# Two filler tiles in SBUF: the operands of TensorE at multiples of 256 bytes

## The chip, the core and the metric

The kernel runs on one core of a Trainium2 chip. The metric is device time in microseconds (us) of one execution; lower is better. The profile shows one execution, taken by the hardware profiler.

## What is computed

Block-causal attention over 4 x 8 heads of 576 positions, then two feed-forward stages over all 2304 tokens. Cut to what matters:

```python
# q, k, v: (4, 8, 576, 64) float32
scores = (1/8) * q @ k.T                      # masked where block(i) < block(j), block = 64
attn = exp(scores - max); attn = attn / (sum(attn) + 1e-9)
x = (attn @ v) -> (2304, 512)
x = (1 / (1 + exp(-(x @ w_gate))) * (x @ w_val)) @ w_out     # 512 -> 1536 -> 512
h = x @ w_in;  out = maximum(0.01 * h, h) @ w_out2            # 512 -> 2048 -> 512
```

## The kernel before

Everything is held transposed: features on the 128 partitions, tokens along the free dimension. The feed-forward products are made of float32r matmuls of 128 x 128 weights against up to 512 tokens. For accuracy every operand is split into a high part and a low part, and a product is three matmuls: high by high, high by low, low by high. So each streamed tile and each weight tile `w` holds two halves, and a unit of four 128-row pieces is 12 matmuls into one PSUM tile (L1296 to L1302 in `half_unit`).

The tokens are worked through in three slices. The first has 768 tokens in two parts of 256 and 512; its `x` lies in `xa` (256) and `x0` (512). The second has 512 tokens, in `x1`. The last two slices of 512 run as a pair, by a scheme of seven block products instead of eight (`pair_unit`, L1123), each product being two groups of three matmuls (L1146 to L1150); its streamed blocks lie in whatever is free by then: `both`, `x1`, `xa`, `g`, `qk`, `raw`, `acc` and `sg`. Weights are in `w`, a ring of seven buffers of 4096 bytes in each partition.

Attention of batch 0 comes first, that of the others is interleaved with the feed-forward work of the first two slices. Scores take both operands from `qk` (L426), transposes use `both` and `ident` (L567, L631), and the products with `v` stream the transposed probabilities from `both` (L655). These are full fp32 matmuls, which stand in the trace as two records each.

A planner (`Plan.order`, L149) orders the operations of all engines by due times and by costs that it works out from shapes; it knows no addresses. Rings and single tiles are reserved in the order in which the code opens their pools, from L263 on, each tile rounded up to 32 bytes. `warm` is a tile of one column that serves to load the Exp table early (L1454 to L1456); it is made in the pool `const`, which comes first in memory.

Of the kernel before, what the change touches and what calls it, by code (L numbers as in the profile page):

```python
# [8 lines left out]
F32 = mybir.dt.float32  # L9
# [4 lines left out]
AF = mybir.ActivationFunctionType  # L14
# [4 lines left out]
P = 128  # L19
# [205 lines left out]
def block_attention_then_two_mlps(  # L225
# [13 lines left out]
    nc = tc.nc  # L239
# [16 lines left out]
    def pool(name, bufs, **k):  # L256
        return ctx.enter_context(tc.tile_pool(name=name, bufs=bufs, **k))

    def ring(name, bufs, shape, dtype=F32, **k):
        return Ring(pool("p_" + name, bufs, **k), bufs, shape, dtype, name)  # L260

    out_hbm = out
    const = pool("const", 1)  # L263
# [20 lines left out]
    ident = const.tile([P, P], F32, name="ident")  # L284
    mask = const.tile([P, 4 * P + BLK], BF16, name="mask")
    x1 = const.tile([P, 4, 2, TN], F32R, name="x1")
    r_x = ring("x0", 4, [P, 2 * TN])
    r_xa = ring("xa", 2, [P, 4 * CUT])
    x0, xa, xt = [r_x.tile(F32R) for _ in range(4)], [r_xa.tile(F32R) for _ in range(2)], []
# [1159 lines left out]
    with tc.manual_schedule():  # L1449
        make_identity(nc, ident)  # L1450
        nc.gpsimd.memset(p_l[BLK:, (NKT - 1) * P:], 0.0)
        nc.gpsimd.memset(mask, 0.0)
        nc.gpsimd.memset(mask[:BLK, 4 * P:], MASK)
        warm = const.tile([P, 1], F32, name="warm")  # L1454
        nc.vector.memset(warm, 0.0)
        nc.scalar.activation(warm, warm, AF.Exp)  # L1456
        for o, e in plan.order():
            for t in o.uses:
                if t.ap is None:
                    t.ap = t.ring.pool.tile(t.ring.shape, t.dtype, name=t.ring.name)  # L1460
            if o.either:
                o.fn(e)
            else:
                o.fn()
# [39 lines left out]
```

## Time and profile before

| | us |
|---|---|
| median of 3 runs (lowest, highest) | 995.12 (994.21, 996.48) |
| the profiled execution | 994.91 |
| its span | 993.1 |
| TensorE busy | 977.9 |
| TensorE's weight loads busy | 779.7 |
| VectorE busy | 779.5 |
| ScalarE busy | 550.3 |
| GpSimd busy | 166.1 |

A matmul's end is modelled in this profile, and matmuls overlap: one lasts longer than the distance to the next. How fast TensorE goes is read from the starts, so the rows below are mostly of the timeline, which gives the start of a group of like matmuls, the time from its first start to its last end, and their number.

### The profile page before, as it was taken

The page shows a single profiled execution, that of the slowest core. Times are in us where ns is not written, and L with a number is a line of the kernel's source. Part 1 is how long each engine was busy: PE and PEld are TensorE (multiplying, and loading weights), DVE is VectorE, ACT ScalarE, POOL GpSimd, SP SyncE. Part 2 cuts the span into 40 slices and gives each one's busy share as a digit, 9 for nine tenths or more (in the row PEclk, how much of TensorE's full clock was granted, in tenths as well). Part 3 has the DMA queues.
Part 4 walks back from the last instruction along what each step waited for, and adds up shares of the span by engine and source line. Part 5 has one row for each costly group of instructions (what it writes and reads, how often), then busy time and mean ns, then how long its engine had stood idle before and what let it go on. Part 6 is the DMA issues. An engine that isn't in the chain of part 4 may idle for free.

```text
span 993.1 us, 15675 instructions
## 1 busy us (share of the span) xinstructions
PE 977.9 (98%) x5468; PEld 779.7 (79%) x5468; DVE 779.5 (78%) x1658; ACT 550.3 (55%) x1103; POOL 166.1 (17%) x172
## 2 busy tenths in 40 slices
PE   7999999999999999999999999999999999999998
PEld 4688888878888878778777777788888877888886
DVE  6989989889989847777689888966437489958656
ACT  7988776676766526464566565443525144643521
POOL 2422001221102001232332223021002021100000
PEclk9999999999999999999999999999999999999999
DMA  8499786756876537979997877876565555665554
GB/s 207 135 292 270 264 289 219 258 186 242 265 258 197 208 116 268 299 273 298 281 296 266 303 265 243 280 267 220 173 200 186 187 170 160 204 204 182 193 185 154
DMA packets 92718, 227.52 MB, mean 229 GB/s; under 512 B 9952, under 2 KB 29920, under 8 KB 92640
## 3 DMA queue, kind: packets, MB, share of 16 engines
q1 hardware_dynamic: 92640, 226.53, 69.5%
q8 instruction: 43, 0.70, 0.3%
q14 instruction: 35, 0.29, 0.1%
HBM read 150.47 MB, written 76.02 MB: 228 GB/s over the span
## 4 chain that ended last, share of the span: by engine, by line
PE 94%; DVE 3%; DMA 1%; ACT 1%; SPq 0%; issue 0%; POOL 0%; DVEq 0%; ACTq 0%
PE mm L1299 48%; PE sc L1147 17%; PE tp L1147 9%; PE mm L1147 4%; PE tp L631 3%; PE sc L426 3%; PE pa L655 2%; PE tp L426 2%; PE tp L567 1%; DMA qk<-in_qk 1%; PE mm L655 1%; PE tp L582 1%; DMA w<-ds 1%; DVE x L1219 0%; SPq L330 0%; DVE g L353 0%
## 5 line engine op out<-in xcount | busy, mean ns | idle before, releaser
L1299 PE MATMUL mm<-x,w 128*128 128x512 f32 (+2 forms) x1008 | 236.9, 387 | 0.0
L1299 PEld LDWEIGHTS mm<-x,w 128*128 128x128 f32 x1008 | 179.8, 188 | 40.8 <-issue 5.2
L1299 PE MATMUL mm<-g,w 128*128 128x512 f32 (+1 forms) x792 | 164.0, 358 | 0.0
L1299 PEld LDWEIGHTS mm<-g,w 128*128 128x128 f32 x792 | 130.0, 189 | 23.4 <-issue 2.3
L1147 PE MATMUL sc<-both,w 128*128 128x512 f32 x480 | 130.6, 396 | 0.1
L1147 PEld LDWEIGHTS sc<-both,w 128*128 128x128 f32 x480 | 90.1, 188 | 21.8 <-ACT wf L340 0.5
L498 ACT ACTIVATE both<-both,nm 128x256 f32<-128x256 f32 (+5 forms) x148 | 84.1, 570 | 29.7 <-DVE nm L483 29.1
L899 POOL TENSOR_TENSOR wf<-mag,rnd 128x512 int32<-128x512 int32 x28 | 37.4, 1335 | 204.3 <-DVE w L353 149.5
L885 ACT ACTIVATE mag<-raw 128x512 f32<-128x512 f32 x68 | 45.5, 670 | 43.9 <-DVE wf L899 18.0
L1299 PE MATMUL mm<-xa,w 128*128 128x256 f32 x480 | 62.7, 281 | 0.0
L1299 PEld LDWEIGHTS mm<-xa,w 128*128 128x128 f32 x480 | 59.9, 188 | 3.3 <-issue 0.8
L353 DVE TENSOR_TENSOR g<-gf,g 128x512 fp32r<-128x512 f32 (+2 forms) x73 | 57.8, 793 | 3.5 <-ACT g L340 3.4
L518 POOL TENSOR_SCALAR both<-both,r 128x256 f32<-128x256 f32 (+6 forms) x54 | 34.9, 652 | 116.4 <-DVE r L511 97.0
L340 ACT ACTIVATE g<-gf 128x512 fp32r<-128x512 f32 (+2 forms) x61 | 40.0, 657 | 23.6 <-DVE gf L1330 11.9
L516 ACT ACTIVATE both<-both,r 128x384 f32<-128x384 f32 (+6 forms) x94 | 48.6, 566 | 6.9 <-DVE r L511 6.9
L483 DVE CUSTOM_DVE_ANT_0 both<-sc,mask 128x256 f32<-128x256 f32 (+6 forms) x101 | 39.4, 423 | 15.9 <-PE sc L426 15.8
L1360 DVE TENSOR_TENSOR acc<-mm,acc 128x512 f32<-128x512 f32 (+1 forms) x60 | 35.7, 598 | 18.1 <-PE mm L1299 17.7
L1219 DVE TENSOR_TENSOR x<-sc,x 128x512 f32<-128x512 f32 x44 | 30.2, 689 | 23.2 <-PE sc L1147 23.2
L426 PE MATMUL sc<-qk 64*128 64x384 f32 (+5 forms) x228 | 42.2, 415 | 5.9 <-DMA qk<-in_qk 5.9
L893 DVE SCALAR_TENSOR_TENSOR mag<-raw,mag 128x512 int32<-128x512 int32 x68 | 47.4, 698 | 0.3
L1299 PE MATMUL mm<-sg,w 128*128 128x512 f32 (+1 forms) x216 | 47.4, 355 | 0.0
L353 DVE TENSOR_TENSOR w<-wf,w 128x512 fp32r<-128x512 f32 x68 | 46.5, 684 | 0.2
(255 smaller groups left out, 1851.0 us busy)
## 6 DMA issues: line engine op xcount, KB each, us to landing
w<-wd SPq DMA_DIRECT2D x102, 512.0 KB, 4.6
raw<-in_w SPq DMA_DIRECT2D x68, 512.0 KB, 4.5
wd<-w SPq DMA_DIRECT2D x68, 512.0 KB, 4.2
ds<-raw SPq DMA_DIRECT2D x68, 512.0 KB, 5.2
w<-ds SPq DMA_DIRECT2D x68, 512.0 KB, 4.3
qk<-in_qk SPq DMA_DIRECT2D x32, 288.0 KB, 6.3
w<-wd SPq DMA_DIRECT2D x68, 128.0 KB, 3.8
v<-in_v SPq DMA_DIRECT2D x32, 160.0 KB, 3.5
```

Of the source, the lines that this page charges most:

```text
L340: nc.scalar.activation(dst(), src(), AF.Copy)
L353: engines[e].tensor_tensor(dst(), a(), f32(b()), ALU.subtract)
L426: nc.tensor.matmul(ps[row:row + nq, col:col + nk], lhsT=tqk[half, 0, q0:q0 + nq], rhs=tqk[half, 1, k0:k0 + nk], start=True, stop=True,)
L483: nc.vector.tensor_tensor_reduce(out=pt[:, n:n + width], in0=ps[:, col:col + width], in1=mask[:, 4 * P + BLK - width:] if masked else mask ...
L498: nc.scalar.activation(pt[:, :n], pt[:, :n], AF.Exp, bias=nm[:, k - 1:k], scale=-1.0, accum_out=sm[:, i:i + 1],)
L516: nc.scalar.activation(pt[:, :n], pt[:, :n], AF.Copy, scale=r[:, i:i + 1])
L885: op("act", c_act(n), lambda: nc.scalar.activation(mag[:], words(1).bitcast(F32), AF.Abs), [raw], [mag], [raw, mag], d - 8)
L893: op("dve", c_dve(n), lambda: nc.vector.scalar_tensor_tensor(out=mag[:].bitcast(I32), in0=words(1).bitcast(I32), scalar=-0x40000000, in1=m ...
L899: engines[e].tensor_tensor(wf[:].bitcast(I32), mag[:].bitcast(I32), rnd[:], ALU.add)
L1147: nc.tensor.matmul(p[:, :n], lhsT=wt[:, wl, at * P:(at + 1) * P], rhs=view[:, xl], start=first and k == 0 and wl + xl == 0, stop=k == 1 an ...
L1299: nc.tensor.matmul(ps[:, :n], lhsT=ws[:, wl, k * P:(k + 1) * P], rhs=srcs[k]()[:, xl, hs], start=k == 0 and wl + xl == 0, stop=k == 3 and ...
L1360: op("dve", c_dve(n), lambda: nc.vector.tensor_tensor(a(), ps[:, :n], a(), ALU.add), [ps], toks_a, [ps, *host], e)
```

## The change

`warm` grows from 1 column to 64 (from 4 bytes, rounded to 32, to 256) and is made right after `x1`, where it stood already in memory. A new tile `even` of 48 columns (192 bytes), which nothing reads or writes, stands between the small rings `nm`, `sm`, `r` and the ring `x0`: its pool is opened there. No instruction is added, taken away or moved; the two that use `warm` name its first column.

```diff
     ident = const.tile([P, P], F32, name="ident")
     mask = const.tile([P, 4 * P + BLK], BF16, name="mask")
     x1 = const.tile([P, 4, 2, TN], F32R, name="x1")
+    warm = const.tile([P, 64], F32, name="warm")
+    pool("even", 1).tile([P, 48], F32, name="even")
     r_x = ring("x0", 4, [P, 2 * TN])
...
-        warm = const.tile([P, 1], F32, name="warm")
-        nc.vector.memset(warm, 0.0)
-        nc.scalar.activation(warm, warm, AF.Exp)
+        nc.vector.memset(warm[:, :1], 0.0)
+        nc.scalar.activation(warm[:, :1], warm[:, :1], AF.Exp)
```

Where the tiles start in a partition (byte, and its residue modulo 256):

| tile | before | residue | after | residue |
|---|---|---|---|---|
| `last`, `ident`, `mask` | 16512, 19072, 19584 | 128 | the same | 128 |
| `x1` | 20736 | 0 | 20736 | 0 |
| `raw`, `mag`, `rnd`, `wf` | from 37152 | 32 | from 37376 | 0 |
| `w` | from 63776 | 32 | from 64000 | 0 |
| `g`, `gf` | from 92448 | 32 | from 92672 | 0 |
| `qk`, `v` | from 126240 | 32 | from 126464 | 0 |
| `x0`, `xa` | from 145760 | 96 | from 146176 | 0 |
| `sg`, `both`, `acc` | from 170336 | 96 | from 170752 | 0 |

Within these tiles the operands start at multiples of 256 bytes, save for the second half of the last queries' scores in batch 0 (column 288), so a tile's residue is that of its operands.

## Rows read from the trace of the kernel before

**Rows 1.** The page, span and busy time of each engine (share of the span, instructions):

```profile
span 993.1 us, 15675 instructions
...
PE 977.9 (98%) x5468; PEld 779.7 (79%) x5468; DVE 779.5 (78%) x1658; ACT 550.3 (55%) x1103; POOL 166.1 (17%) x172
```

**Rows 2.** The page, the chain that ended last, by engine:

```profile
PE 94%; DVE 3%; DMA 1%; ACT 1%; SPq 0%; issue 0%; POOL 0%; DVEq 0%; ACTq 0%
```

**Rows 3.** Busy time by stretch: first slice, second slice, paired stage:

```profile
core 0: us, PE busy (x) PEld busy (x) DVE busy (x) ACT busy (x) POOL busy (x), PEclk, DMA share, GB/s
...
60.00:364.00 304.00, 303.65 (x1982) 257.87 (x1982) 263.71 (x597) 200.67 (x406) 39.68 (x34) 1.00 0.71 237
364.00:655.00 291.00, 289.87 (x1616) 220.81 (x1613) 243.24 (x521) 163.88 (x331) 77.82 (x81) 1.00 0.81 271
655.00:985.00 330.00, 328.28 (x1413) 264.44 (x1412) 221.75 (x346) 135.69 (x225) 29.38 (x22) 1.00 0.59 193
```

**Rows 4.** Waits of TensorE, longest first: total us, times, longest:

```profile
PE sc L426 <- DMA qk<-in_qk: 5.9, 3, 4.6
PE tp L1147 <- DMA w<-ds: 1.1, 1, 1.1
...
PE pa L426 <- DMA qk<-in_qk: 0.2, 1, 0.2
```

**Rows 5.** Weight loads by line and shape: count, busy us, mean ns, idle before:

```profile
L1299 PEld LDWEIGHTS mm<-x,w 128*128 128x128 f32 x1008 | 179.8, 188 | 40.8 <-issue 5.2 <-ACT gf L1343 0.3 <-DVE mag L889 0.2
L1147 PEld LDWEIGHTS sc<-both,w 128*128 128x128 f32 x480 | 90.1, 188 | 21.8 <-ACT wf L340 0.5 <-DVE v L1180 0.3 <-DVE x L1219 0.3
```

**Rows 6.** Timeline, paired stage: start us, us, engine, line, names, shapes, count:

```profile
723.99 0.85 PE L1147 MATMUL sc<-qk,w 128*128 128x512 f32 x3
724.67 0.84 PE L1147 MATMUL tp<-g,w 128*128 128x512 f32 x3
725.35 0.84 PE L1147 MATMUL sc<-raw,w 128*128 128x512 f32 x3
726.03 0.84 PE L1147 MATMUL sc<-qk,w 128*128 128x512 f32 x3
726.71 0.84 PE L1147 MATMUL mm<-raw,w 128*128 128x512 f32 x3
727.39 0.86 PE L1147 MATMUL sc<-acc,w 128*128 128x512 f32 x3
```

**Rows 7.** Timeline, paired stage, with `both` and `xa` streamed:

```profile
746.81 0.87 PE L1147 MATMUL sc<-both,w 128*128 128x512 f32 x3
747.51 0.86 PE L1147 MATMUL tp<-xa,w 128*128 128x512 f32 x3
748.21 0.86 PE L1147 MATMUL sc<-both,w 128*128 128x512 f32 x3
748.91 0.86 PE L1147 MATMUL tp<-xa,w 128*128 128x512 f32 x3
```

**Rows 8.** First slice, a run from `g`: timeline, then lengths min/median/max:

```profile
232.23 5.83 PE L1299 MATMUL mm<-g,w 128*128 128x512 f32 x25
...
L1299 PE MATMUL mm<-g,w x22: 389/389/389, 232.7 to 237.4; 128*128 128x512 f32 x22
```

**Rows 9.** Second slice, a run from `x1`: timeline, then lengths min/median/max:

```profile
375.20 5.52 PE L1299 MATMUL mm<-x,w 128*128 128x512 f32 x23
...
L1299 PE MATMUL mm<-x,w x22: 392/395/397, 375.4 to 380.3; 128*128 128x512 f32 x22
```

**Rows 10.** Timeline, first slice, a run from `x0`:

```profile
246.08 3.14 PE L1299 MATMUL mm<-x,w 128*128 128x512 f32 x13
```

**Rows 11.** Timeline, first slice, runs of 256 columns:

```profile
191.43 1.48 PE L1299 MATMUL mm<-g,w 128*128 128x256 f32 x11
...
103.69 1.34 PE L1299 MATMUL mm<-xa,w 128*128 128x256 f32 x10
...
259.29 1.07 PE L1299 MATMUL mm<-xa,w 128*128 128x256 f32 x8
```

**Rows 12.** Timeline, first slice, a unit from `g` right after 256 columns:

```profile
192.87 2.91 PE L1299 MATMUL mm<-g,w 128*128 128x512 f32 x12
```

**Rows 13.** Attention's transposes and products with `v`: count, busy us, mean ns:

```profile
L631 PE MATMUL tp<-ident,both 128*128 128x128 f32 x304 | 42.8, 274 | 0.8 <-ACT both L340 0.8
...
L655 PE MATMUL pa<-both,v 128*64 128x384 f32 (+3 forms) x192 | 26.2, 415 | 0.0
L567 PE MATMUL tp<-ident,both 128*128 128x128 f32 (+1 forms) x80 | 13.2, 276 | 0.3 <-ACT both L340 0.2
L655 PE MATMUL mm<-both,v 128*64 128x256 f32 (+1 forms) x96 | 10.4, 352 | 0.4 <-DVE both L342 0.3
```

## The prediction

> **What bounds the kernel now.** I read the busy line first, then the chain that ended last, the stretches, and TensorE's own waits. TensorE is busy 977.9 us of a span of 993.1 us [rows 1], the chain runs through it for 94% [rows 2], and its granted clock is 1.00 in every stretch [rows 3]. Its longest wait is the first load of q and k (5.9 us); every other wait that the view lists is at most 1.1 us [rows 4]. So the end is set by how many matmuls there are and by how closely they follow each other. The change adds none and moves none, so only the second can move.
>
> The change touches addresses alone, and the question is whether the trace shows an address in the distance from one matmul to the next (the pitch). It does, and this is the core of the argument. A row of the timeline that merges n matmuls covers n-1 pitches and the length of the last one. Before the change all weight tiles `w` lie at residue 32 (the byte in the partition, modulo 256), while the streamed operands lie at three residues:
>
> - `g`, `raw`, `qk` at 32, the same as `w`. From 723.99 on, five groups of three matmuls start exactly 0.68 us apart while the streamed tile goes from `qk` to `g`, `raw`, `qk` and `raw` [rows 6], so 226.7 ns each. The run of 25 from `g` gives the same: (5.83 - 0.39)/24 = 226.7, with every length at 389 ns [rows 8].
> - `both` and `xa` at 96, the same distance from `w`. Their groups start 0.70 us apart [rows 7], so 233.3 ns.
> - `x0`, also at 96: (3.14 - 0.39)/12 = 229.2 ns [rows 10]. So residue 96 has more than one settled pitch.
> - `x1` at 0, the only streamed buffer that is aligned already: (5.52 - 0.395)/22 = 233.0 ns [rows 9], with lengths of 392 to 397 ns.
>
> The weight loads last 188 ns under all of these [rows 5], so a load is not what became longer. Each lies inside a matmul's pitch, and its read of `w` runs beside the read of the streamed tile. What separates the good buffers from the others is that they lie a multiple of 256 bytes from `w`. `qk` is the useful case: its second half starts 2304 bytes after its first, which is 256 modulo 512, and it still runs at 0.68 us a group. So agreement modulo 256 is enough.
>
> **The change part by part.** The larger `warm` and the new `even` cost no instruction: the memset and the one Exp still work on one column. They take 640 bytes of each partition, and nothing is queued anew, so both are priced at 0. The order of instructions on every engine is the same.
>
> What they do is to bring `w`, `g`, `raw`, `qk`, `x0`, `xa`, `sg`, `both` and `acc` to residue 0, where `x1` lies. All streamed operands of the split products then agree with `w` modulo 256, as `g`, `raw` and `qk` do today. My forecast takes that agreement to be what counts, and prices every matmul as `g` behaves now. `g` does not reach 226.7 at once: after a switch of width its pitches are 233, 236, 229, 232, 231, 227 and then 226.7, and the row of twelve shows the mean, (2.91 - 0.39)/11 = 229.1 ns [rows 12]. That costs some 28 ns a restart, and I charge it to each.
>
> - Paired stage, 655 to 985 us, 1413 matmuls [rows 3]. From the starts of all of them, 1404 pitches are under 250 ns and sum to 324.8 us, a mean of 231.4; between 226.7 [rows 6] and 233.3 [rows 7] the mix of buffers gives about that. TensorE is hardly interrupted here, so nearly all settle: 1404 x (226.8 - 231.4) = **-6.4 us**.
> - Second slice, 364 to 655 us. 431 such pitches stream `x1`, at a mean of 233.2; attention work cuts into most units, so `g`'s mean with restarts (228.3) is what they get: 431 x -4.9 = -2.1 us. `g`, `sg` and `xa` together lose another 0.8 us. **-2.9 us**.
> - First slice, 60 to 364 us. It alternates between 256 and 512 columns. At 256 columns the settled pitch is (1.48 - 0.28)/10 = 120 ns for `g`, (1.34 - 0.28)/9 = 118 for `xa`, and elsewhere (1.07 - 0.28)/7 = 113 for the same `xa` [rows 11]. So agreement with `w` is no gain at this width, and the restart at each switch takes what 512 columns would win: `g` needs 1.43 + 2.75 us for a pair of units and `x0` with `xa` 1.41 + 2.75. **-0.5 us**, in truth nothing. If the 113 became the rule here, this term would be -6.5.
> - Attention's own matmuls in full fp32. Scores take both operands from `qk`, so their distance stays. Products of probabilities with `v` go from 64 apart to a multiple of 256, and transposes from 32 apart (`ident` at 128, `both` at 96) to 128. The trace has no equal shapes at two distances here. The large groups of these add up to 42.8 + 26.2 + 13.2 + 10.4 = 92.6 us [rows 13]; at the ratio of 233.3 to 226.7, 2.9%, that is 2.7 us either way, and the sign is open. I take 0, since rows 7 and 10 show that a distance alone doesn't fix the pitch.
> - Transfers and the other engines meet shifted addresses as well. No row separates these by residue. TensorE waits for transfers 5.9 + 1.1 + 0.2 = 7.2 us [rows 4]; a quarter of it, 2 us either way, is the bound, and I take 0.
>
> Sum: -6.4 - 2.9 - 0.5 = -9.8 us on TensorE. Not all of it reaches the end. In the first two slices VectorE is busy 87% and 84% [rows 3], and a faster TensorE will meet its results later. I take off 1.5 us, half of what is won there, and get -8.3. The profiled execution took 994.91 us for its span of 993.1, and the median of the runs is 995.12, so the two agree to 0.2 us and the forecast is **986.8 us**, 0.8% faster.
>
> The distance between two operands should by one rule not matter at all. The Trainium skill, TensorE: Matmul & The Clock Gate, section "Step-by-step: what each phase is for", says that "Loading the next tile's weights doesn't steal SBUF read bandwidth from the running matmul", since the two have a read port each. Rows 6 to 10 show pitches that differ by buffer, so something in the addresses acts; by that rule it would have to be the streamed buffer's own address, and that is the second rival below.
>
> **The rivals.** *Own address (slower).* If the streamed operand's own residue sets the pitch, then 32 is good, 96 middling and 0 the worst, and the change moves everything to 0. For this: `x1` is the one aligned buffer and runs at 233.0 [rows 9]. Against it: pitches keep changing for some six matmuls after a change of buffer or a restart [rows 12], and `x0` and `both` have the same residue with 229 and 233 [rows 7, 10], so a second stream is in play. Its price is each stretch at 233.2 ns for 512 columns: 1404 x 1.8 = +2.5, the second slice +1.4, the first +2.3, together +6.2 us: **1001 us**. It decides as soon as more than about half of the 512-column matmuls settle at `x1`'s pitch.
>
> *Nothing changes.* Several settled pitches exist per distance, so the new common distance may settle on another of them, or on a mixture whose mean is the present 231: **995 us**, 2 us either way. The Trainium skill, SBUF — State Buffer, in the note on cachelines under "Door 1: The DMA port swizzle", knows lines of 16 bytes only, and all buffers stand at a multiple of 16 already, so by it the filler does nothing. The pitches by residue [rows 6 to 10] speak against that as the whole story. That the tiles do not land where they should can be excluded: every address in the changed kernel is a multiple of 256 except for `ident`, `last` and `mask`, which stay at 128.
>
> *Eaten by the others.* TensorE gains 9.8 us, but in the first two slices all of it is waited away, and a third of the paired stage's share as well: -6.4 x 2/3 = -4.3, so **991 us**. For it: VectorE's 87%. Against it: waits that TensorE shows now are almost none [rows 4].
>
> **How the numbers follow.** The forecast has a chance of 0.57, eaten by the others 0.10, nothing changes 0.13, own address 0.20. About 0.2%, or 2 us, is what a measurement of this kernel can tell from no change. Faster by more is 0.57 + 0.10 = 0.67, within 0.13, slower 0.20. The forecast's own range is 982 to 991 us: -8.3 with 2.7 for attention and 2 for transfers on either side. To leave out no more than two in ten, the range has to reach into the slower case: 981 to 1000 leaves out some 0.04 below and 0.12 above.
>
> **What would show it.** In the paired stage, groups of three should start 0.68 us apart whatever they stream, and matmuls from `both`, `xa` and `x` should last 389 ns instead of 396; in the second slice settled runs from `x` should show 226.7. If they show 233 everywhere, `g` and `raw` too, then own address was right. If the pitches fall and the span doesn't, the waits of TensorE will have grown. The forecast is wrong altogether if agreement modulo 256 was only a by-product of residue 32, or if the pitch settles at a third value. The weight load should stay at 188 ns.

## The result

The changed kernel takes 986.67 us, median of 4 runs (985.49 to 987.15), beside 995.65 us of the kernel before; the ratio is 0.991, 95% interval 0.9892 to 0.9927. The forecast was 986.8. The kernel before had a median of 995.12 us of three runs when the forecast was made, and the fourth run moved it to 995.65; so the change measured is 9.0 us, where 8.3 were forecast.

The page of the changed kernel answers [rows 1]: TensorE is busy 9.4 us less with the same number of matmuls, and the span is 9.4 us shorter.

```profile
span 983.7 us, 15675 instructions
...
PE 968.5 (98%) x5468; PEld 780.4 (79%) x5468; DVE 777.4 (79%) x1658; ACT 549.6 (56%) x1103; POOL 163.1 (17%) x172
```

Busy time by stretch, columns as in [rows 3]. The stretches begin and end at the same matmuls as those of before, and so lie a little earlier:

```profile
59.10:363.90 304.80, 304.45 (x1983) 259.15 (x1983) 263.80 (x597) 200.86 (x406) 39.65 (x34) 1.00 0.71 236
363.90:652.00 288.10, 286.30 (x1616) 220.95 (x1613) 241.64 (x521) 163.51 (x331) 75.00 (x81) 1.00 0.81 274
652.00:975.80 323.80, 322.21 (x1412) 264.13 (x1411) 221.33 (x346) 135.31 (x225) 29.26 (x22) 1.00 0.61 197
```

The first slice went from 304.0 to 304.8 us, the second from 291.0 to 288.1, the paired stage from 330.0 to 323.8. Ahead of them stand 59.1 us instead of 60.0, behind them 7.9 instead of 8.1. The first of these is the wait for the first loads, which differs from execution to execution: a second profile of the changed kernel has 59.8 there.

The timeline of the paired stage, first the stretch of [rows 6], then that of [rows 7]:

```profile
719.12 0.84 PE L1149 MATMUL sc<-qk,w 128*128 128x512 f32 x3
719.80 0.84 PE L1149 MATMUL tp<-g,w 128*128 128x512 f32 x3
720.48 0.84 PE L1149 MATMUL sc<-raw,w 128*128 128x512 f32 x3
721.16 0.84 PE L1149 MATMUL sc<-qk,w 128*128 128x512 f32 x3
721.84 0.84 PE L1149 MATMUL mm<-raw,w 128*128 128x512 f32 x3
722.52 0.84 PE L1149 MATMUL sc<-acc,w 128*128 128x512 f32 x3
```

```profile
741.56 0.84 PE L1149 MATMUL sc<-both,w 128*128 128x512 f32 x3
742.24 0.84 PE L1149 MATMUL tp<-xa,w 128*128 128x512 f32 x3
742.92 0.84 PE L1149 MATMUL sc<-both,w 128*128 128x512 f32 x3
743.60 0.84 PE L1149 MATMUL tp<-xa,w 128*128 128x512 f32 x3
```

All groups now start 0.68 us apart, `both` and `xa` too, which were 0.70 apart. The group from `acc`, which lasted 0.86 us before, lasts 0.84 like the others. In the second slice the run from `x1` [rows 9] has settled as well, with all lengths at 389 ns and (6.28 - 0.389)/26 = 226.6 ns from start to start:

```profile
374.70 6.28 PE L1301 MATMUL mm<-x,w 128*128 128x512 f32 x27
...
L1301 PE MATMUL mm<-x,w x27: 389/389/389, 374.7 to 380.6; 128*128 128x512 f32 x27
```

TensorE's waits, answering [rows 4], hardly differ: 1.0 us more for `w`, 0.8 less for the first loads, and every other one under 1 us.

```profile
PE sc L428 <- DMA qk<-in_qk: 5.1, 2, 4.8
PE tp L1149 <- DMA w<-ds: 2.1, 2, 1.6
```

The weight loads beside 512 columns last what they lasted [rows 5]:

```profile
L1301 PEld LDWEIGHTS mm<-x,w 128*128 128x128 f32 x1008 | 179.9, 188 | 38.5 <-issue 5.2 <-ACT gf L1345 0.3 <-DVE mag L891 0.2
```

### The profile page after: what moved, and what is told of

Same layout as the page of the kernel before. It is cut to its first block, busy times and chain, and to the rows that moved or that the text cites. A ratio compares the mean times of both kernels' runs of the same rounds, so it can differ in the third digit from the quotient of the medians.

```text
span 983.7 us, 15675 instructions
## 1 busy us (share of the span) xinstructions
PE 968.5 (98%) x5468; PEld 780.4 (79%) x5468; DVE 777.4 (79%) x1658; ACT 549.6 (56%) x1103; POOL 163.1 (17%) x172
## 4 chain that ended last, share of the span: by engine, by line
PE 94%; DVE 2%; ACT 2%; DMA 1%; issue 0%; SPq 0%; ACTq 0%; DVEq 0%
PE mm L1301 47%; PE sc L1149 18%; PE tp L1149 9%; PE mm L1149 4%; PE tp L633 3%; PE sc L428 3%; PE pa L657 2%; PE tp L428 2%; PE tp L569 1%; DMA w<-ds 1%; PE mm L657 1%; PE tp L584 1%; ACT both L500 1%; ACT both L518 1%; DVE x L1221 0%; DMA qk<-in_qk 0%
## 5 line engine op out<-in xcount | busy, mean ns | idle before, releaser
L1301 PE MATMUL mm<-x,w 128*128 128x512 f32 (+2 forms) x1008 | 234.2, 384 | 0.0
L1149 PE MATMUL sc<-both,w 128*128 128x512 f32 x480 | 128.2, 390 | 0.1
```

The costliest lines, as they stand in the source:

```text
L1149: nc.tensor.matmul(p[:, :n], lhsT=wt[:, wl, at * P:(at + 1) * P], rhs=view[:, xl], start=first and k == 0 and wl + xl == 0, stop=k == 1 an ...
L1301: nc.tensor.matmul(ps[:, :n], lhsT=ws[:, wl, k * P:(k + 1) * P], rhs=srcs[k]()[:, xl, hs], start=k == 0 and wl + xl == 0, stop=k == 3 and ...
```

## The experiments

The theory is that the distance from `w` to the streamed tile (start of the streamed tile less start of `w`, modulo 256) sets the pitch (A). Against it stood that the residue of one of them does: of the weights (W) or of the streamed buffer. All edits below are against the changed kernel; times are medians, ratios are against the kernel before in the same session. "Settled" means pitches of the tenth and later matmuls of an uninterrupted run at one width and one distance; they are worked out from the starts in each trace. A matmul's length in these traces is the pitch behind it and some 162 ns (389 for 227, 395 for 232, 404 for 241), so it says the same as the pitch and isn't a second witness.

**Each filler alone.** First `even` without the larger `warm`:

```diff
-    warm = const.tile([P, 64], F32, name="warm")
+    warm = const.tile([P, 1], F32, name="warm")
```

> Half of the change: the tile even alone, warm stays one column. The streamed buffers x0, xa, sg, both, acc come to residue 32, where w, g, raw and qk stay; x1 stays alone at 0. Theory A (the distance between the streamed tile and w, modulo 256): everything but x1 settles at 226.7 ns; x1 stays at 233 and unsettles its neighbours in the paired stage: 990 to 992 us. Theory W (only the weights' own residue 0 counts): w is still at 32, so no gain, 995 us.

Measured 992.06 us, ratio 0.9958 (0.9945 to 0.997), just above the 990 to 992 us that A gave. The gain without `w` at a multiple of 256 speaks against W. The timeline of the paired stage shows `x1` as the one that stays behind, and its neighbour still unsettled:

```profile
745.67 0.86 PE L1149 MATMUL mm<-x,w 128*128 128x512 f32 x3
746.37 0.85 PE L1149 MATMUL sc<-both,w 128*128 128x512 f32 x3
747.06 0.84 PE L1149 MATMUL tp<-xa,w 128*128 128x512 f32 x3
747.74 0.84 PE L1149 MATMUL sc<-both,w 128*128 128x512 f32 x3
```

`x1` takes 0.70 us for its three, the first `both` after it 0.69, then it is 0.68.

Then the larger `warm` without `even`:

```diff
-    pool("even", 1).tile([P, 48], F32, name="even")
```

> The other half: warm of 64 columns alone, no tile even. w, g, raw, qk go to residue 0, where x1 is; x0, xa, sg, both and acc go from 96 to 64. Theory A: x1 agrees with w now and settles at 226.7 ns, both and xa stay at a distance of 64 and at 229 to 233: 990 to 992 us. Theory W: w is at 0, so the whole gain, 986.7 us.

Measured 992.73 us, ratio 0.9971 (0.996 to 0.9982), a little less gain than A gave, and not the whole that W asked for. `both` and `xa` at a distance of 64 take 0.69 us a group here:

```profile
744.97 0.85 PE L1148 MATMUL tp<-xa,w 128*128 128x512 f32 x3
745.66 0.85 PE L1148 MATMUL sc<-both,w 128*128 128x512 f32 x3
746.35 0.85 PE L1148 MATMUL tp<-xa,w 128*128 128x512 f32 x3
```

Settled, distance 0 has 226.8 ns and 64 has 230.0 in this kernel. The two halves give 0.42% and 0.29%, less than the 0.9% of both together. Where two distances follow each other, even the good one restarts: with the larger `warm` alone the pitches at distance 0 average 229.8 ns, in the changed kernel 227.7.

**Nothing at a multiple of 256, all at one distance.**

```diff
+    const.tile([P, 8], F32, name="shift")
     x1 = const.tile([P, 4, 2, TN], F32R, name="x1")
```

> The changed kernel with a tile of 32 bytes ahead of x1, so that w and every streamed buffer, x1 too, lie at residue 32: nothing at a multiple of 256, all at a distance of 0 modulo 256. Theory A: as the changed kernel, 986.7 us within 1.5, x1 at 226.7 ns. Theory W, or any theory in which it is the multiple of 256 that counts: the gain is lost, 995 us or more.

Measured 987.52 us, ratio 0.9915 (0.9902 to 0.9929): the whole gain, with every one of these buffers at residue 32. The settled pitch is 226.67 ns, and `x1` at residue 32 has the lengths that it has at 0:

```profile
L1302 PE MATMUL mm<-x,w x14: 389/389/389, 377.0 to 379.9; 128*128 128x512 f32 x14
```

The multiple of 256 is not what counts.

**Only `w` moved,** with all streamed buffers left at multiples of 256:

```diff
+    pool("ahead", 1).tile([P, 8], F32, name="ahead")
     r_w = ring("w", 7, [P, 2, 4 * P], F32R)
+    pool("behind", 1).tile([P, 56], F32, name="behind")
```

> The changed kernel with the seven weight buffers alone moved to residue 32 (32 bytes ahead of their ring, 224 behind); all streamed buffers stay at 0. Theory A: each 512-column matmul is at x1's old distance and settles at 233 ns: 3012 x 6.5 ns is about 16 to 19 us over the changed kernel with restarts being no dearer, so 1000 to 1005 us, slower than before. A theory of the streamed buffer's own residue: no loss, 986.7 us.

Measured 1002.82 us, ratio 1.0068 (1.0054 to 1.0081): slower than before the change, with every streamed buffer at a multiple of 256. The settled pitch over 1940 matmuls is 233.34 ns, that of `x1` before. `g`, which had 389 ns in [rows 8], lasts 395 in its runs, and the weight loads still 188:

```profile
L1303 PE MATMUL mm<-g,w x19: 395/395/396, 235.8 to 240.0; 128*128 128x512 f32 x19
...
L1303 PEld LDWEIGHTS mm<-x,w 128*128 128x128 f32 x1008 | 179.8, 188 | 42.1 <-issue 5.1 <-ACT gf L1347 0.3 <-DVE mag L893 0.2
```

So the distance is the cause, and residues by themselves are not.

**Which distances are good.** The same edit with 16, 24, 32 and 48 columns ahead of the ring of `w`, and 64 less that number behind.

> The changed kernel with w alone at residue 128, all streamed buffers at 0. If the distance counts modulo 128, it is as good as the changed kernel: 226.7 ns, 986.7 us. If it counts modulo 256, the 512-column pitch settles between 229 and 233 ns: 994 to 1002 us.

> The changed kernel with w alone at residue 192, so that each streamed buffer lies 64 past it modulo 256, the distance of x0, xa, sg, both and acc before. If only the distance counts, 512 columns settle at 229 to 233 ns and 256 columns at 113 to 118: 992 to 998 us. If the absolute residue mattered beside it, the pitches of before (229.98 and 230.3 settled on average) would not come back.

> The changed kernel with w alone at residue 64: streamed buffers lie 192 past it, or 64 ahead. If the sign of the distance doesn't count, it behaves like the run with w at 192, 992 to 998 us; if the pitch grows with the distance modulo 256 (0: 226.7, 64: 230, 224: 233.3), it is 1000 to 1003 us.

> The changed kernel with w alone at residue 96, a distance of 160. If odd multiples of 32 are all alike (as 224 was, 233.3 ns), it takes 1001 to 1004 us, as the run with w at 32 did; if the pitch depends on the size of the distance, some value of its own between 990 and 1003.

| `w` at residue | distance | 512 columns, all under 250 ns / settled | 256 columns, settled | us | ratio (interval) |
|---|---|---|---|---|---|
| 0 (the changed kernel) | 0 | 227.7 / 226.7 | 120.0 | 986.67 | 0.991 (0.9892 to 0.9927) |
| 192 | 64 | 229.2 / 228.9 | 117.2 | 990.32 | 0.9949 (0.9934 to 0.9963) |
| 128 | 128 | 232.6 / 232.5 | 119.1 | 999.77 | 1.0046 (1.0031 to 1.0061) |
| 96 | 160 | 234.2 / 234.3 | 118.1 | 1003.94 | 1.0087 (1.0072 to 1.0102) |
| 64 | 192 | 233.2 / 233.3 | 114.1 | 999.34 | 1.0039 (1.0025 to 1.0054) |
| 32 | 224 | 233.2 / 233.3 | 118.7 | 1002.82 | 1.0068 (1.0054 to 1.0081) |

The lengths in a settled run from `x1` (min/median/max) rise and spread in the same way, here at distances of 64, 128, 160 and 192:

```profile
L1303 PE MATMUL mm<-x,w x24: 388/392/394, 375.7 to 380.9; 128*128 128x512 f32 x24
...
L1303 PE MATMUL mm<-x,w x24: 390/393/404, 376.5 to 381.9; 128*128 128x512 f32 x24
...
L1303 PE MATMUL mm<-x,w x23: 392/397/400, 380.7 to 385.8; 128*128 128x512 f32 x23
...
L1303 PE MATMUL mm<-x,w x21: 393/393/398, 373.1 to 377.8; 128*128 128x512 f32 x21
```

The distance doesn't count modulo 128, since 128 isn't as good as 0. It need not be 0 modulo 512: `x1` in the changed kernel lies 256 past `w` by that measure and settles at 226.6. The sign counts (64 and 192 differ). Odd multiples of 32 are not all alike: 160 settles at 234.3 ns and 224 at 233.3, though by time alone, with ratios whose intervals overlap, they couldn't be told apart. The run at 64 missed its range on the good side: with one distance throughout it settles at 228.9, where 64 among others gave 230 to 233. The run at 192 came in just under its 1000 us, and no steady growth with the distance is left to expect: 160 is the worst, not 224. And 256 columns follow another order: 192 is their best, 0 their worst.

**A use of that.** In the first slice `xa` is streamed 256 columns at a time. This kernel puts it 192 past `w` there, and leaves it at 0 in the paired stage:

```diff
-    r_xa = ring("xa", 2, [P, 4 * CUT])
+    r_xa = ring("xa", 2, [P, 4 * CUT + 64])
...
-        a, c = (x[:].rearrange("p (k l n) -> p k l n", l=2, n=n) for x, n in ((xa[k // 2], CUT), (x0[k], TN)))
+        a, c = (x[:, at:at + m].rearrange("p (k l n) -> p k l n", l=2, n=n) for x, at, m, n in ((xa[k // 2], 48, 4 * CUT, CUT), (x0[k], 0, 2 * TN, TN)))
```

> The changed kernel with one thing more: in the first slice the 256-column tiles of x (xa) lie 192 bytes past w modulo 256, the distance at which 256 columns settled at 114 ns instead of 120; the paired stage still uses xa from its start, at a distance of 0. If the pitch follows the distance for each matmul, some 430 pitches of 256 columns fall from 121.5 to 117 or less, 1.9 to 2.5 us: 984.2 to 984.8. If changing the distance at each switch of width costs a new settling in the 512 columns that follow, the gain goes: 986 to 988.

> The changed kernel once more, on the chip and beside the runs of the one with xa moved: 986.7 us within 1, whichever theory holds.

Measured 985.91 us (985.36 to 986.63), beside 987.22 (986.43 to 988.1) of the changed kernel on the same chip; the ratios are 0.9903 (0.989 to 0.9917) and 0.9919 (0.9905 to 0.9932). The intervals overlap, so the two are not told apart by them; the timelines of the first slice tell the sign. First the changed kernel, then this one:

```profile
115.33 1.60 PE L1301 MATMUL mm<-xa,w 128*128 128x256 f32 x12
116.76 2.91 PE L1301 MATMUL mm<-x,w 128*128 128x512 f32 x12
119.51 1.60 PE L1301 MATMUL mm<-xa,w 128*128 128x256 f32 x12
```

```profile
116.38 1.58 PE L1301 MATMUL mm<-xa,w 128*128 128x256 f32 x12
117.79 2.88 PE L1301 MATMUL mm<-x,w 128*128 128x512 f32 x12
120.51 1.58 PE L1301 MATMUL mm<-xa,w 128*128 128x256 f32 x12
```

A pair of units takes 4.13 us instead of 4.18, and the first slice 303.2 instead of 304.8. The mean pitch of `xa` fell from 121.9 to 119.9 ns, 0.9 us for 432 of them, and that of the 512 columns from `x0` from 228.8 to 227.7, 0.5 us for 398. So the expectation of 1.9 to 2.5 us from `xa` was too high: it settled at 117.5 ns here, not at 114. One distance among others settles otherwise than the same distance throughout; why is not shown.

**Whose weights.** The load of the next matmul's weights runs beside the running matmul: in this trace it starts 2 to 4 ns after it, for 2884 of 2955 matmuls of 512 columns. Is it that load whose address counts, or the matmul's own weights, loaded earlier? Here the buffers of `w` lie at 0 and 128 by turns:

```diff
-    r_w = ring("w", 7, [P, 2, 4 * P], F32R)
+    r_w = ring("w", 7, [P, 8 * P + 32], F32R)
+    pool("behind", 1).tile([P, 32], F32, name="behind")
...
                     t.ap = t.ring.pool.tile(t.ring.shape, t.dtype, name=t.ring.name)
+                    if t.ring.name == "w":
+                        t.ap = t.ap[:, :8 * P].rearrange("p (l n) -> p l n", l=2)
```

> The changed kernel with the seven buffers of w by turns at residues 0, 128, 0, 128, 0, 128, 0; all streamed buffers at 0. In a settled run of whole units (12 matmuls of one weight buffer each), the first matmul that leaves 226.7 ns tells whose distance counts. Theory N (the load that runs beside the matmul, the next one's weights): already the last matmul of a unit at 0 that is followed by one at 128 is off. Theory O (the matmul's own weights): that one is still at 226.7, and the first of the unit at 128 is off. Time under either: between the changed kernel and the one with all of w at 128, 991 to 997 us, nearer to the middle or above it, since every change of buffer unsettles some six matmuls.

Measured 995.63 us, ratio 1.0007 (0.9997 to 1.0017). The unit from 376.71 has its weights at 0 and the next unit's lie at 128. Lengths by min/median/max, first up to its eleventh matmul (with the last of the unit ahead), then its twelfth and the first of the next unit:

```profile
L1302 PE MATMUL mm<-x,w x12: 389/389/389, 376.5 to 379.0; 128*128 128x512 f32 x12
...
L1302 PE MATMUL mm<-x,w x2: 396/400/404, 379.2 to 379.4; 128*128 128x512 f32 x2
```

The twelfth matmul, its own weights at 0, is already at 396 ns, and the start after it comes after 233 ns instead of 227. It is the same in the whole trace, whose matmuls match those of the program one to one, so that each one's addresses are known. Where the four pitches ahead were 226 or 227 ns, the last pitch of a buffer at 0 before one at 128 is 232 or 233 in all 31 uninterrupted cases, and before another buffer at 0 it is 226 or 227 in all 40. So the weights that count are those of the next matmul. The unit at 128 then goes on with 241, 232, 231, 232, 228 and 230 ns, and back at 0 it takes some seven more matmuls to settle.

**Which streamed tile** they meet, the one running or the one to come, can be read from the run with `even` alone. There `w` stays at one residue, and `x1`, 224 past it, comes after tiles at a distance of 0. Where the pitches ahead had settled, the last matmul ahead of `x1` keeps 226 or 227 ns in all 40 cases, and the first from `x1` takes 234 or 235. One of them:

```profile
L1301 PE MATMUL mm<-g,w x4: 389/389/389, 656.9 to 657.6; 128*128 128x512 f32 x4
...
L1149 PE MATMUL tp<-x,w x3: 395/397/397, 657.8 to 658.3; 128*128 128x512 f32 x3
```

So the distance that counts is that between the tile which the running matmul streams and the weights that are loaded beside it for the next one.

## Why the prediction was right, step by step

**The reading of the rows** held. The forecast took agreement with `w` modulo 256 to be what separates 226.7 from 233 ns, from `g`, `raw` and `qk` against `both`, `xa` and `x1`. The runs with all at 32 and with `w` alone at 32 show this as cause. *Own address*, the slower rival, falls with them: streamed tiles at residue 0 are fast or slow depending on where `w` is. Its price of 1001 us was near what the same kernel costs when only `w` is out of step (1002.82). *Nothing changes* falls with the result, and *eaten by the others* with TensorE's waits, which hardly grew.

The rule that was weighed there, the Trainium skill's "TensorE: Matmul & The Clock Gate", section "Step-by-step: what each phase is for", that loading the next weights takes no read bandwidth from the running matmul, doesn't agree with this kernel's traces: the address of the next load alone moves a pitch from 227 to 233 ns.

**Paired stage:** -6.4 forecast, 330.0 - 323.8 = 6.2 us less measured. **Second slice:** -2.9 forecast, 291.0 - 288.1 = 2.9 us less measured, pitches and restarts together. One reading behind this term was off: in the trace of before `g` averages 229.4 ns there, not 228.3, and with 229.4 the term of `x1` would have been -1.6 instead of -2.1. Measured, `x1` came to 227.9 ns, and `g` itself to 228.4: `x1` gave 2.4 us and the other buffers 0.5, where 2.1 and 0.8 were forecast. That the sum was met is in part luck.

**First slice:** -0.5 forecast, +0.8 measured: this term was mis-sized. I priced 256 columns at a flat 120 ns and called that no loss. With their restarts, 720 such pitches went from 120.0 to 121.6 ns, 1.1 us more, while 512 columns won 0.5. Agreement with `w` is the worst of the tried distances for 256 columns, which the three values of [rows 11] hinted at and the sum left out.

**What the others would eat:** 1.5 us taken off (half of what the sum wins in the first two slices would have been 1.7), and nothing of it was seen. The second slice gave its 2.9 in full, and VectorE, there busy 243.24 us before [rows 3] and 241.64 after, met the earlier matmuls in time. The two errors, 1.3 us too low in the first slice and 1.5 too high here, nearly cancel: 0.8 - 2.9 - 6.2 = -8.3, the forecast's own sum, by another way. The rest of the 9.4 us between the two profiles lies ahead of the slices and behind them. The hit on 986.67 is therefore closer than the working deserves.

**Attention and transfers** at 0: the steps from one matmul of attention to the next add up to 0.3 us less in the second slice and to the same in the first, inside the bound of 2.7. Of transfers nothing can be told beyond the first loads, which vary by more than 1 us between executions (the first slice begins at 59.1 in one trace, at 61.4 in that with all at 32).

**The signs named ahead** came: 0.68 us a group whatever is streamed, 389 ns from `both`, `xa` and `x`, 226.6 in the settled run from `x1`, loads at 188 ns. The filler takes 416 bytes more of each partition, by the table of addresses, and not 640; nothing hangs on that.

## What to carry to other kernels

Where float32r matmuls follow each other with a new weight load each, look at the start-to-start times by streamed buffer: different settled values for the same shape point to addresses, not to work. Put the weight ring and the streamed tiles at the same residue modulo 256 when the matmuls have 512 columns; the residue itself is free, mixing distances costs restarts, and a shorter matmul may want another distance. Check that after every change to tile sizes, since a few small tiles ahead of a ring shift all that follows.

## What was not expected

- The pitch has a memory. After a break or a change of distance some six to ten matmuls run at 224 to 240 ns before it settles. At distance 0 it settles on one value, 226 or 227 ns each time; at the others mostly on a cycle that repeats, worked out from the starts: of 226, 229 and 232 ns at 64, of 231 and 236 at 192, and of seven pitches from 228 to 241 at 128. And one distance can settle on several values: 64 gave 228.9 throughout one kernel and 230.3 on average in the kernel before, and `xa` at 192 settled at 117.5 ns where the same distance gave 114.1.
- 256 columns have 120.0 ns at a distance of 0 and 114.1 at 192, in the opposite order of 512 columns (226.7 and 233.3).
- A distance costs more than the change gained: between the best (986.67 us) and the worst place of `w` (1003.94) lie 17 us, 1.8%.

What stays open: why 256 and 512 columns differ in order, and how and where the two reads meet. Distances of 32 and 96, and steps below 32 bytes, weren't tried.
